# One operand sum of a seven-product matrix multiply, from GpSimd to VectorE in two halves

## Chip, cores and metric

One core of a Trainium2 chip. The metric is device time in microseconds (us) of one launch, the median of several runs; lower is better.

## What is computed

Pooled-query attention, then a gated feed-forward layer, all from the reference:

```python
q_pool = q.reshape(B, H, S // 2, 2, D).mean(axis=3)        # B=H=8, S=1152, D=64
scores = scale * q_pool @ k^T ;  attn = softmax(scores) ;  x = attn @ v     # 4608 rows of 512
a = x @ w1 ; b = x @ w2                                    # 512 -> 1024 each
h = a * b @ w3 ; out = h @ w_out                           # 1024 -> 1024 -> 512
```

## The kernel before, in words

**Attention.** Heads go in 32 pairs. The scores of all pairs are one long row of columns, cut into 324 groups of 512 for both heads of a pair (`scores`, L423 to L437): TensorE writes a group into one of three PSUM buffers (tag `psc`), ScalarE takes its exponential into the ring `ring` (L437). 144 "AV" units (`av_mm`, L463; `av_norm`, L484 to L498) multiply the exponentials with v and divide by the sums, on TensorE and VectorE. `prepare` (L779), called once for each pair, puts a batch of four GpSimd instructions in that engine's queue: the casts and sums of k (L344), q (L348, L350) and v (L357). GpSimd works its queue in order, and so does VectorE.

**Feed-forward.** The two last weights are multiplied once into T (1024 x 512). The 4608 rows then go in nine chunks of 512 (`moe_groups`). For each chunk, 16 projections (`proj`, L578, alternately by w1 and w2) and their gates (L695) fill the tile gT: [128 partitions, 8 feature tiles, 512 rows] in fp16. gT times T is done with seven products of half-size blocks instead of eight. With the four blocks of gT (feature tiles 0-3 or 4-7, rows 0-255 or 256-511) named a11, a12, a21, a22, each 1024 columns wide in a partition, the left operands are

- s1 = a21 + a22, by VectorE, four instructions of 256 columns, one after each of the last four gates (L608)
- a21 becomes a11 - a21, by GpSimd, four instructions beside those (L609)
- a11 becomes s1 - a11, **the second operand sum**, one instruction of 1024 columns (L616), by GpSimd, and by VectorE only where `tail[0]` is set, that is in the last two chunks
- a12 becomes a12 - a11, one instruction of 1024 columns by GpSimd (L618)

The products (L678, eight matmuls each) run in the order 1, 2, 5, 6, 7, 4, 3. Product 1 reads the old a11, 2 the old a12, 5 reads s1, 6 the new a11, 7 the new a21, 4 reads a22, 3 the new a12. The result of each leaves PSUM through VectorE (`only` L641, `plus` L632; in the last two chunks `only` runs on ScalarE, L639), and two sums of results follow on GpSimd (L635).

**Order.** The projections and products are "fills", put between the attention work by hand. The 324 score groups make 108 visits of three. Each visit is three score groups on TensorE and then a string of items found by a search (`_visits`, L192): "A" is an AV unit, "m" a fill that goes into the single PSUM bank `mo`, "s" a fill that takes one of the three score buffers, "P" a transpose. The search tracks TensorE, ScalarE and VectorE with fixed costs; GpSimd is not in it. The list `fills` (L821 to L828) says for each fill how many PSUM-to-SBUF steps' worth of VectorE time it brings beyond the normal one (third entry). What is left after visit 108 runs as AV unit, fill, AV unit, fill and so on, and the two last chunks run alone as the tail.

The steps that the change touches: `s_rest` (L611), its calls in `done` (L650) after products 1 and 2, and the entries of `fills` for a chunk.

Of the kernel before, what the change touches and what calls it, by code (L numbers as in the profile page):

```python
# [11 lines left out]
ALU = mybir.AluOpType  # L12
# [244 lines left out]
def kernel(  # L257
# [11 lines left out]
    nc = tc.nc  # L269
# [7 lines left out]
    NF = dff // 128  # L277
# [243 lines left out]
    tail = [False]  # L521
# [34 lines left out]
    HF, HM, HC = NF // 2, dm // 2, 256  # L556
    TB = {}

    def t_sums():
        b11, b12 = T16[:, 0:HF, 0:HM], T16[:, 0:HF, HM:dm]  # L560
        b21, b22 = T16[:, HF:NF, 0:HM], T16[:, HF:NF, HM:dm]
        ts = msb.tile([128, 4, HF, HM], FP16, tag="wo", bufs=1, name="tsum")
        for o, x, y in ((0, b12, b11), (1, b22, ts[:, 0]), (2, b22, b12), (3, b21, ts[:, 1])):
            nc.gpsimd.tensor_tensor(out=ts[:, o], in0=x, in1=y, op=ALU.subtract)
        TB.update({1: b11, 2: b21, 3: b22, 4: ts[:, 3], 5: ts[:, 0], 6: ts[:, 1], 7: ts[:, 2]})
# [9 lines left out]
    def proj(pw, wt, ft, c):  # L575
        for mc in range(NC):
            for (d0, a, n) in runs(c):
                nc.tensor.matmul(pw[:, d0:d0 + n], wt[:, mc, ft * 128:ft * 128 + 128], xT[:, mc, a:a + n],  # L578
                                 start=(mc == 0 and d0 == 0), stop=(mc == NC - 1), skip_group_check=True)

    def store(eng, pos, osb):
        b, r = pos // (2 * Sq) * 2, pos % (2 * Sq)
        if r == QM * 128:
            for u in range(2):
                r0 = (b + u) * Sq + QM * 128
                eng.dma_start(out=out[r0:r0 + QT, :], in_=osb[u * QT:u * QT + QT, :])
            return
        if r > QM * 128:
            b, r = b + 1, r - QM * 128 - 2 * QT
        eng.dma_start(out=out[b * Sq:b * Sq + QM * 128, :].rearrange("(p c) n -> p c n", c=QM)[:, r // 128, :], in_=osb)  # L590
# [3 lines left out]
    def moe_groups(c):  # L594
        t = {}

        def left(n):
            g = t["g"]
            lo, hi = slice(0, HC), slice(HC, CH)
            return {1: g[:, 0:HF, lo], 2: g[:, HF:NF, lo], 3: g[:, HF:NF, lo], 4: g[:, HF:NF, hi],  # L600
                    5: t.get("s1"), 6: g[:, 0:HF, lo], 7: g[:, 0:HF, hi]}[n]

        def s_pair(f):
            g = t["g"]
            if f == 0:
                t["s1"] = msb.tile([128, HF, HC], FP16, tag="s1", bufs=1, name="s1")
            a11, a21, a22 = g[:, f, 0:HC], g[:, f, HC:CH], g[:, HF + f, HC:CH]
            nc.vector.tensor_tensor(out=t["s1"][:, f], in0=a21, in1=a22, op=ALU.add)  # L608
            nc.gpsimd.tensor_tensor(out=a21, in0=a11, in1=a21, op=ALU.subtract)  # L609

        def s_rest(n):  # L611
            g = t["g"]
            a11, a12 = g[:, 0:HF, 0:HC], g[:, HF:NF, 0:HC]
            if n == 2:
                eng = nc.vector if tail[0] else nc.gpsimd
                eng.tensor_tensor(out=a11, in0=t["s1"], in1=a11, op=ALU.subtract)  # L616
            else:
                nc.gpsimd.tensor_tensor(out=a12, in0=a12, in1=a11, op=ALU.subtract)  # L618

        IS = 1.0 / (SCL * SCL)  # L620

        def part(name):
            t[name] = msb.tile([128, 2, HM], FP32, tag="t2k", bufs=4, name=name)
            return t[name]

        def rows(h):
            if h not in t:
                t[h] = msb.tile([128, 2, dm], FP32, tag="osb", bufs=2, name="osb")
            return t[h]

        def plus(out, pt, x):
            nc.vector.scalar_tensor_tensor(out=out, in0=pt, scalar=IS, in1=x, op0=ALU.mult, op1=ALU.add)  # L632

        def add(out, x, y):
            nc.gpsimd.tensor_tensor(out=out, in0=x, in1=y, op=ALU.add)  # L635

        def only(out, pt):
            if tail[0]:
                nc.scalar.mul(out=out, in_=pt, mul=IS)  # L639
            else:  # L640
                nc.vector.tensor_scalar_mul(out=out, in0=pt, scalar1=IS)  # L641

        def out_rows(h, u):
            if tail[0]:
                eng = nc.scalar if c in final and u else nc.sync
            else:
                eng = nc.gpsimd
            store(eng, c * CH + h * HC + u * 128, rows(h)[:, u, :])

        def done(n, pt):  # L650
            if n == 1:
                only(part("p"), pt)
                s_rest(2)
            elif n == 2:
                plus(rows(0)[:, :, 0:HM], pt, t["p"])
                s_rest(4)
            elif n == 5:
                only(part("q"), pt)
            elif n == 6:
                plus(t["p"], pt, t["p"])  # L660
                add(part("w"), t["p"], t["q"])
            elif n == 7:
                plus(part("z"), pt, t["p"])
                add(rows(1)[:, :, HM:dm], t["z"], t["q"])
            elif n == 4:
                plus(rows(1)[:, :, 0:HM], pt, t["z"])
                for u in range(2):
                    out_rows(1, u)
            else:
                for u in range(2):  # L670
                    plus(rows(0)[:, u, HM:dm], pt[:, u, :], t["w"][:, u, :])
                    out_rows(0, u)

        def product(pt, n, tiles=(0, 1)):
            a, b = left(n), TB[n]
            for u in tiles:
                for f in range(HF):
                    nc.tensor.matmul(pt[:, u, :], a[:, f, u * 128:u * 128 + 128], b[:, f, :],  # L678
                                     start=(f == 0), stop=(f == HF - 1))

        def first(pa, ft):
            if ft == 0:
                t["g"] = msb.tile([128, NF, CH], FP16, tag="g8", bufs=2, name="gT")
            proj(pa, w1sb, ft, c)

        def keep(pa):
            t["a"] = msb.tile([128, CH], FP32, tag="t2k", bufs=4, name="asb")
            if tail[0]:
                nc.scalar.copy(out=t["a"], in_=pa)  # L689
            else:  # L690
                nc.vector.tensor_copy(out=t["a"], in_=pa)  # L691

        for ft in range(NF):
            def gate(pb, ft=ft):
                nc.vector.tensor_tensor(out=t["g"][:, ft, :], in0=pb, in1=t["a"], op=ALU.mult)  # L695
                if ft >= HF:
                    s_pair(ft - HF)
                if ft == 0 and not TB:
                    t_sums()

            yield 1, lambda pa, ft=ft: first(pa, ft), keep, 0.0
            yield 1, lambda pb, ft=ft: proj(pb, w2sb, ft, c), gate, 0.0
        order7 = (1, 2, 5, 6, 7, 4, 3)
        for i, n in enumerate(order7):
            def go(po, n=n, i=i):
                near[0] = c in final and i >= 3
                product(po.rearrange("p (u m) -> p u m", u=2), n)

            def put(po, n=n):
                done(n, po.rearrange("p (u m) -> p u m", u=2))  # L710

            def go_last(po, n=n):
                for u in range(2):
                    pu = ps.tile([128, 2, 512], FP32, tag="psc", bufs=3, name="mol")[:, 0:2, 0:HM]
                    product(pu, n, (u,))
                    plus(rows(0)[:, u, HM:dm], pu[:, u, :], t["w"][:, u, :])
                    out_rows(0, u)

            if c in final and c == max(final) and n == order7[-1]:
                yield 1, go_last, None, 0.0  # L720
            else:
                yield 1, go, put, 0.0
# [28 lines left out]
    def w_load(dst, src):  # L751
# [7 lines left out]
        out=ident16, in_=ident16, compare_op=ALU.not_equal, fill=1.0,  # L759
# [46 lines left out]
    for c in range(B * Sq // CH):  # L806
        n = 0
        for b in range(B):
            for t in range(NT5):
                if xpos(b, t) < (c + 1) * CH and xpos(b, t) + (128 if t < QM else QT) > c * CH:  # L810
                    p = b * HP + HP - 1
                    i = unit_of(p, t)
                    n = max(n, i + 2, index[(p, QM - 1)] + 1 + HELD if p >= XD and t < QM else 0)
# [7 lines left out]
    fills = []  # L821
# [2 lines left out]
    free = []  # L824
    for n in range(NU + 1):
        for c in loose.get(n, []):
            fills += [(1, 0.0, 0.0)] * NF + [(1, 0.0, 0.0), (1, 0.0, 0.25)] * HF + [(1, 0.0, 0.0)] * 7
        free.append(len(fills))  # L828
    turn = {}
    for p in range(1, NPE):  # L830
# [121 lines left out]
```

## Time and profile before

| | |
|---|---|
| median of three runs | 420.89 us (420.61 to 423.12) |
| the profiled execution | 420.94 us, of which span 419.2 us |
| second operand sum L616 on GpSimd | 7 x 2.12 us, at 102.2 to 362.0 us |
| second operand sum L616 on VectorE | 2 x 0.69 us, at 386.4 and 406.6 us |
| L618 on GpSimd | 9 x 2.12 us |
| L608 on VectorE (256 columns) | 36 x 0.292 us (0.291 to 0.367) |
| L609 on GpSimd (256 columns) | 36 x 0.667 us |
| a GpSimd batch L344, L348, L350, L357 | 1.15, 1.27, 0.45 and 1.14 us |
| a VectorE step out of PSUM (L641, L632, L695) | 0.69 us |
| a product of eight matmuls | 0.87 us of TensorE, start to start |

How to read it: the span runs from the first to the last instruction of the program. A view of the profile is the page (sums), the waits (which engine waited for which, in total, number of times, longest), or the timeline (instructions in order: start, busy time, engine, line, operation, and in brackets the idle time of the engine before it and what ended it).

### The profile page before, as it was taken

Reading aid. Unit: us, or ns where it says so; the run is one execution under the profiler, and the core shown is the slowest. Engines: PE = TensorE matmul, PEld = TensorE weight load, DVE = VectorE, ACT = ScalarE, POOL = GpSimd, SP = SyncE. Lnnn points to the kernel's source line nnn. Section 1 sums busy time; section 2 is a strip of 40 time slices with the busy share of each in tenths; the row PEclk is TensorE's granted clock in tenths of the full one; section 3 lists DMA queues with packets and bytes.
Section 4 is the critical chain, followed back from the end, with each engine's and each line's share of the span. In section 5 each row is a group of like instructions: output and inputs, shape, how many; then the busy total and the mean of one; then the engine's idle time right before and its main releaser. Section 6 shows DMA issues by size and latency. Waiting matters only on the chain.

```text
span 419.2 us, 13307 instructions
## 1 busy us (share of the span) xinstructions
PE 394.9 (94%) x5545; PEld 268.1 (64%) x5545; DVE 236.3 (56%) x643; ACT 322.0 (77%) x347; POOL 253.9 (61%) x284
## 2 busy tenths in 40 slices
PE   3899999999999999999999999979998999989992
PEld 1477786566766676658666866567776755745561
DVE  1156665666565655565556555745564556765552
ACT  4988988998899898989998989869996896023230
POOL 5899868937971689069906890598158501522333
PEclk9999999999999999999999999999998999999997
DMA  8999998499799999979999999699976420030302
GB/s 272 250 316 317 299 295 302 156 278 262 200 315 269 253 174 284 232 210 244 301 252 278 225 255 255 174 270 242 311 118 111 95 80 14 14 114 1 100 2 107
DMA packets 90963, 86.39 MB, mean 206 GB/s; under 512 B 59664, under 2 KB 64272, under 8 KB 90896
## 3 DMA queue, kind: packets, MB, share of 16 engines
q1 hardware_dynamic: 81600, 59.32, 58.8%
q0 software_dynamic: 8720, 25.10, 20.9%
q10 hardware_dynamic: 576, 1.05, 0.7%
q8 instruction: 44, 0.72, 0.7%
q14 instruction: 23, 0.19, 0.2%
HBM read 67.11 MB, written 9.44 MB: 183 GB/s over the span
## 4 chain that ended last, share of the span: by engine, by line
PE 85%; DVE 4%; POOL 3%; ACT 3%; issue 2%; DMA 1%; POOLq 1%; ACTq 0%; DVEq 0%
PE psc L432 19%; PE avb L463 16%; PE mot L578 16%; PE mo L578 14%; PE mot L678 5%; PE mo L678 5%; ACT ring L437 3%; PE mo L545 3%; PE avb L460 2%; PE ptk L372 2%; DVE gT L695 1%; POOL gT L616 1%; DMA qst<-in_q_dram 1%; PE mot L545 1%; DVE kqT L374 1%
## 5 line engine op out<-in xcount | busy, mean ns | idle before, releaser
L437 ACT ACTIVATE ring<-psc 128x1024 f16<-128x1024 f32 x324 | 308.1, 1025 | 38.8 <-PE psc L432 37.6
L609 POOL TENSOR_TENSOR gT<-gT 128x256 f16<-128x256 f16 x36 | 24.0, 667 | 129.3 <-DVE s L608 71.3
L432 PE MATMUL psc<-kqT 64*128 64x512 f16 (+7 forms) x1152 | 96.5, 291 | 4.5 <-ACT ring L437 1.5
L463 PEld LDWEIGHTS <-ring 128*128 128x128 f16 x2304 | 84.8, 98 | 21.3 <-issue 8.9
L463 PE MATMUL avb<-vaug,ring 128*128 128x65 f16 x2304 | 91.8, 194 | 0.2
L432 PEld LDWEIGHTS <-kqT 64*128 64x128 f16 x1152 | 46.3, 95 | 31.9 <-issue 9.3
L678 PEld LDWEIGHTS <-gT 128*128 128x128 f16 x432 | 40.3, 98 | 13.5 <-POOL gT L616 4.9
L578 PEld LDWEIGHTS <-w1sb 128*128 128x128 f16 x320 | 28.3, 98 | 30.9 <-issue 6.7
L484 DVE RECIPROCAL rzall<-avb 128x2 f32<-128x2 f32 x144 | 23.8, 165 | 40.2 <-PE avb L463 21.5
L578 PEld LDWEIGHTS <-w2sb 128*128 128x128 f16 x320 | 28.3, 98 | 28.3 <-issue 4.6
L578 PE MATMUL mot<-xT,w2sb 128*128 128x512 f16 (+1 forms) x196 | 42.2, 344 | 0.0
L578 PE MATMUL mot<-xT,w1sb 128*128 128x512 f16 x156 | 40.0, 379 | 1.5 <-DVE z L632 1.5
L348 POOL TENSOR_TENSOR kq<-qst 128x512 f16<-128x512 f32 x31 | 39.4, 1271 | 1.4 <-DMA qst<-in_q_dram 1.4
L695 DVE TENSOR_TENSOR gT<-mot,asb 128x512 f16<-128x512 f32 x41 | 28.4, 692 | 18.3 <-PE mot L578 18.0
L689 ACT COPY asb<-mot 128x512 f32<-128x512 f32 x16 | 9.4, 585 | 37.9 <-PE mot L578 20.1
L344 POOL CAST kq<-kst 128x1152 f16<-128x1152 f32 x31 | 35.6, 1148 | 3.8 <-DMA kst<-in_k_dram 3.3
L357 POOL CAST vaug<-vst 128x1152 f16<-128x1152 f32 x32 | 36.6, 1143 | 0.5 <-DMA vst<-in_v_dram 0.5
L691 DVE COPY asb<-mo 128x512 f32<-128x512 f32 x33 | 22.8, 691 | 24.5 <-PE mo L578 24.3
L695 DVE TENSOR_TENSOR gT<-mo,asb 128x512 f16<-128x512 f32 x31 | 21.4, 692 | 25.7 <-PE mo L578 25.6
L578 PE MATMUL mo<-xT,w1sb 128*128 128x512 f16 (+2 forms) x164 | 34.2, 339 | 0.0
L578 PE MATMUL mo<-xT,w2sb 128*128 128x512 f16 x124 | 32.0, 381 | 0.0
L498 DVE TENSOR_TENSOR xb<-avb,rzall 128x128 f16<-128x128 f32 x96 | 28.0, 292 | 3.3
(100 smaller groups left out, 421.8 us busy)
## 6 DMA issues: line engine op xcount, KB each, us to landing
vst<-in_v_dram SPq DMA_DIRECT2D x25, 576.0 KB, 4.9
kst<-in_k_dram SPq DMA_DIRECT2D x23, 576.0 KB, 5.6
qst<-in_q_dram SPq DMA_DIRECT2D x23, 512.0 KB, 6.7
out_dram<-osb POOLq DMA_DIRECT2D x21, 256.0 KB, 6.1
kst<-in_k_dram POOLq DMA_DIRECT2D x8, 576.0 KB, 9.3
qst<-in_q_dram POOLq DMA_DIRECT2D x8, 512.0 KB, 10.1
vst<-in_v_dram POOLq DMA_DIRECT2D x7, 576.0 KB, 6.6
out_dram<-osb SPq DMA_DIRECT2D x9, 256.0 KB, 2.5
```

The source lines that it names most:

```text
L344: nc.gpsimd.tensor_copy(out=kq16[:, 0:NJ].rearrange("p c u d -> p u c d"), in_=kst.rearrange("p u (c d) -> p u c d", d=D))
L348: eng.tensor_tensor(out=kq16[:, NJ:NJ + QM].rearrange("p c u d -> p u c d"), in0=qv[:, :, :, 0], in1=qv[:, :, :, 1], op=ALU.add)
L357: nc.gpsimd.tensor_copy(out=va[:, :, :, 0:D], in_=vs.pop(p).rearrange("p u (c d) -> p u c d", d=D))
L432: nc.tensor.matmul(psc[:, u, f - s * G:f - s * G + ln], kT2[u * 64:u * 64 + 64, jt, :], qpT[u * 64:u * 64 + 64, i0:i0 + ln], start=True, s ...
L437: nc.scalar.activation(out=ring[:, :, r0:r0 + G], in_=psc, func=AF.Exp, bias=0.0, scale=SCALE)
L463: nc.tensor.matmul(avb[:, o + u * E1:o + u * E1 + E1], ring[:, u, c0:c0 + 128], va[:, u, jt, :], start=(jt == 0 and u == 0), stop=(jt == N ...
L484: nc.vector.reciprocal(out=rzall[:, i, :], in_=av[:, :, D:E1].rearrange("p u o -> p (u o)"))
L498: nc.vector.tensor_tensor(out=xbt, in0=av[:, :, 0:D], in1=rzall[:, i, :].unsqueeze(2).to_broadcast([128, 2, D]), op=ALU.mult)
L578: nc.tensor.matmul(pw[:, d0:d0 + n], wt[:, mc, ft * 128:ft * 128 + 128], xT[:, mc, a:a + n], start=(mc == 0 and d0 == 0), stop=(mc == NC - ...
L609: nc.gpsimd.tensor_tensor(out=a21, in0=a11, in1=a21, op=ALU.subtract)
L678: nc.tensor.matmul(pt[:, u, :], a[:, f, u * 128:u * 128 + 128], b[:, f, :], start=(f == 0), stop=(f == HF - 1))
L695: nc.vector.tensor_tensor(out=t["g"][:, ft, :], in0=pb, in1=t["a"], op=ALU.mult)
```

## The change

The second operand sum of every chunk goes to VectorE as two instructions of 512 columns: feature tiles 0 and 1 after the result of product 1 has been taken, tiles 2 and 3 after that of product 2. L618 is issued behind the second half as before. The planner's list counts more VectorE time for products 1 and 2 (0.45 each) and for the last four gates of a chunk (0.30 in place of 0.25), so that the search gives another order of fills in some visits. The number of visits, and the 173 fills that fall into them, stay.

```diff
         def s_rest(n):
             g = t["g"]
             a11, a12 = g[:, 0:HF, 0:HC], g[:, HF:NF, 0:HC]
-            if n == 2:
-                eng = nc.vector if tail[0] else nc.gpsimd
-                eng.tensor_tensor(out=a11, in0=t["s1"], in1=a11, op=ALU.subtract)
+            if n < 2:
+                h = slice(n * HF // 2, (n + 1) * HF // 2)
+                nc.vector.tensor_tensor(out=a11[:, h], in0=t["s1"][:, h], in1=a11[:, h], op=ALU.subtract)
             else:
                 nc.gpsimd.tensor_tensor(out=a12, in0=a12, in1=a11, op=ALU.subtract)
...
             if n == 1:
                 only(part("p"), pt)
-                s_rest(2)
+                s_rest(0)
             elif n == 2:
                 plus(rows(0)[:, :, 0:HM], pt, t["p"])
+                s_rest(1)
                 s_rest(4)
...
-            fills += [(1, 0.0, 0.0)] * NF + [(1, 0.0, 0.0), (1, 0.0, 0.25)] * HF + [(1, 0.0, 0.0)] * 7
+            fills += [(1, 0.0, 0.0)] * NF + [(1, 0.0, 0.0), (1, 0.0, 0.3)] * HF + [(1, 0.0, 0.45)] * 2 + [(1, 0.0, 0.0)] * 5
```

## The prediction, made before the changed kernel ran

> **What bounds the kernel now.** First the page, for who is busy.
>
> ```profile
> PE 394.9 (94%) x5545; PEld 268.1 (64%) x5545; DVE 236.3 (56%) x643; ACT 322.0 (77%) x347; POOL 253.9 (61%) x284
> PE 85%; DVE 4%; POOL 3%; ACT 3%; issue 2%; DMA 1%; POOLq 1%; ACTq 0%; DVEq 0%
> ```
>
> TensorE is busy for 394.9 of 419.2 us and carries 85% of the chain that ended last; GpSimd (POOL) carries 3%. So a change pays only where TensorE stands still. Next the waits, for whether the moved sum ever holds TensorE:
>
> ```profile
> PEld L678 <- POOL gT L616: 4.9, 2, 2.5
> PE mot L678 <- POOL gT L616: 4.3, 2, 2.3
> ```
>
> The columns are total us, times, longest us. It does, twice: in two of the seven chunks that use GpSimd (weight load and matmul are two views of the same two waits). In the other five nobody waits for L616. Then the timeline of the second, to see why:
>
> ```profile
> 315.82 2.85 ACT L437 ACTIVATE ring<-psc 128x1024 f16<-128x1024 f32 x3 [0.48 <-PE psc L432]
> 315.83 0.67 POOL L609 TENSOR_TENSOR gT<-gT 128x256 f16<-128x256 f16 x1 [2.51 <-DVE rzall L484]
> ...
> 316.44 1.15 POOL L344 CAST kq<-kst 128x1152 f16<-128x1152 f32 x1
> ...
> 319.05 2.86 ACT L437 ACTIVATE ring<-psc 128x1024 f16<-128x1024 f32 x3 [0.37 <-PE psc L432]
> ...
> 319.17 1.14 POOL L357 CAST vaug<-vst 128x1152 f16<-128x1152 f32 x1
> ...
> 320.28 2.11 POOL L616 TENSOR_TENSOR gT<-s,gT 128x1024 f16<-128x1024 f16 x1
> ...
> 322.44 1.86 PE L678 MATMUL mot<-tsum,gT 128*128 128x256 f16 x8 [2.08 <-POOL gT L616]
> ...
> 326.21 5.61 ACT L437 ACTIVATE ring<-psc 128x1024 f16<-128x1024 f32 x6 [4.31 <-PE psc L432]
> ```
>
> The sum L616 is queued on GpSimd behind a whole batch of casts (316.44 to 320.31), and product 6 needs it. The first wait, near 277 us, is the same picture. ScalarE's rows give the price, since each row of three exponentials is one visit: 319.05 to 326.21 is 7.16 us where the visit before took 3.23 (315.82 to 319.05), an excess of 3.93. It is more than the idle time because the eight matmuls behind it took 1.86 us instead of the usual 1.05: the granted clock was 0.53 from 322.4 to 324.3 us and 0.50 in the next microsecond, and 1.00 before. The other visit lasted 5.59 (275.76 to 281.35) against 3.21 for the one before it: 2.38, with the clock at 1.00.
>
> **The change, part by part.** The sum is made against the profiled execution, 420.94 us (span 419.2 and 1.74 around it; the median is 420.89, or 0.05 less).
>
> *The two waits go.* 3.93 + 2.38 = 6.31 us. The visits right behind are some 0.12 shorter than others of their kind (2.73 and 2.83 against 2.85 to 2.95), a catching-up that goes too: 6.31 - 0.25 = 6.06. What is late next there is nothing of size: without these two, TensorE has no gap over 0.3 us from 28 to 368 us, and the sums stand well ahead of product 6 once they need no batch. GpSimd loses 7 x 2.12 = 14.9 us of work; L618 comes forward by up to that 2.12, but product 3, its reader, is the last of seven and waits nowhere now, so that is worth nothing.
>
> *VectorE's own time.* 256 columns take 0.292 (L608) and 1024 take 0.692 (L616 in the tail), so 512 take 0.292 + 256 x 0.400/768 = 0.425. Fourteen halves are 5.95 us more on an engine that is 56% busy. A visit with product 1 holds two PSUM steps (1.38), L608 (0.29), a half (0.43) and one AV unit (0.45) at most, about 2.6 of 3.2 us: it fits, and I cost the bare time at nothing. If the cover failed it would be that 5.95. In the stretch without exponentials (352 to 367 us), where VectorE is at 12.4 of 15 us, its idle pieces between 362 and 366 sum to about 1.2 us against the 0.85 of the two halves.
>
> *VectorE held by GpSimd.* The halves read two SBUF operands, as L608 does. Six times L608 met a running L348; the timeline shows one:
>
> ```profile
> 221.13 1.27 POOL L348 TENSOR_TENSOR kq<-qst 128x512 f16<-128x512 f32 x1
> ...
> 222.18 0.37 DVE L608 TENSOR_TENSOR s<-gT 128x256 f16<-128x256 f16 x1
> 222.36 0.50 POOL L350 TENSOR_TENSOR kq<-qtl 64x128 f16<-64x128 f32 x1
> ```
>
> L608 ended 0.15 us after L348 did (222.55 against 222.40), whenever it had started; so in all six, and L350 took 0.50 instead of 0.45. L900 in the tail, a VectorE instruction beside L635, took 1.384 where its twin L899 took 0.300. So I take it that a half which meets a cast is held to the cast's end and then needs 0.15 + 256 x 0.52 ns = 0.28; a hold is between 0 and 1.27 (a whole L348). The place matters. The changed order puts a batch right behind L609 in chunks 1, 3 and 4 (counting from 0); with the rows of the present trace as clock:
> - Chunk 3: the result of product 1 is taken at 230.97, L348 runs 230.75 to 232.02. First half held to 232.30 (about 0.9), the result step of product 2 to 232.99, second half held by L357 to about 234.1. The changed order puts product 5 right behind 2 in that visit, in `mo`. Behind the halves on VectorE stand the result steps of products 2 and 5 and an AV unit; the third score group waits for the buffer of product 2 (233.06 against 232.5, 0.55), product 6 for `mo` (234.87 against 233.9, 0.97). TensorE loses 1.5.
> - Chunk 1: second half held from 146.88 to 147.48, a score buffer late: 0.2. Chunk 4: halves held 0.1 and 0.2, hidden under an AV unit: 0.
> - Chunk 5: here the changed order puts the batch between the third and the fourth L609, and the second half needs the fourth: a new wait of VectorE for GpSimd. The batch lasts 3.87 (316.44 to 320.31) from the third L609, and the fourth gate comes one visit (3.2) later, so the fourth L609 is some 1.5 late; by then VectorE has two result steps and the first half to do and stands about 0.1 to 0.6: 0.3.
>
> In chunks 0, 2 and 6 no batch meets the halves. Together 2.0 us. Bounds: 0 (all halves fall between casts) and eight halves x 1.27 = 10.2. I take a value near the rows that place them.
>
> *The new order of fills.* No fill leaves or enters the visits, so TensorE's work stays. In four visits two "m" fills now stand around one "s"; from the last matmul to the bank's next one are 0.18 (the usual bracket of L632 behind L678), 0.69 and 0.06 (VectorE's end at 407.26, TensorE's start at 407.32), 0.93, and the fill between takes 0.87: 4 x 0.06 = 0.25. Bounds: 0 and 4 x 0.69.
>
> *The last two chunks.* One sum of 0.69 becomes two of 0.425, the second behind the result step of product 2 and behind the fourth L609 (405.87 to 406.54). The whole sum ended at 407.26 and product 6 stood 0.31 for it. Now its first matmuls can start on the first half, the third needs the second half, which ends at about 407.4 to 407.8. Between -0.3 and +0.5 each; I take +0.1 each, 0.2. L618 follows by the same, with 0.4 to spare before product 3.
>
> Sum: -6.06 + 0 + 2.0 + 0.25 + 0.2 = -3.6; 420.94 - 3.6 = 417.3 us. Without the fills' and the holds' terms it would be 415.1.
>
> A page of the Trainium skill speaks against the change: "SBUF — State Buffer", section "Who interferes with whom", says that a VectorE instruction with two SBUF inputs contends with a GpSimd instruction that reads SBUF, and that the later one is blocked for the whole of the other. By that rule, put on every half near a batch, the sum would be that of the third rival. The six rows of L608 agree with it.
>
> **Rivals.**
> 1. *Nothing is given back*: the halves fall between casts. For it: L608 met a cast in only 6 of 36 cases, and at most 0.075 us was lost. Against: in chunk 3 the half stands in the middle of L348. 420.94 - 6.06 + 0.2 = 415.1.
> 2. *The wait changes its engine*: in chunk 5 VectorE stands for the fourth L609 through the whole batch, with an AV unit and the result step of product 5 behind it, and TensorE waits for their banks. For it: the order, and that a batch has stopped TensorE twice. Against: the batch starts as soon as GpSimd is free, a visit early; its loads kept GpSimd waiting 3.3 us in all (L344, twice). 417.3 + 3.9 = 421.2, no change.
> 3. *Slower: VectorE is held in all eight halves of chunks 1, 3, 4 and 5 by a whole cast*, and TensorE, whose banks VectorE empties, loses it one for one: 420.94 - 6.06 + 10.2 + 0.45 = 425.5. It decides against the change from a mean of 5.6/8 = 0.70 us for each half that reaches TensorE. For it: the batches are unbroken, 3.9 us long. Against: VectorE has idle time in those visits, and in chunk 4 the halves just slip past.
>
> That the change does not do what it says is not a rival: the order has no L616 left on GpSimd.
>
> **How the numbers follow.** Forecast 0.60, rival 1 0.15, rival 2 0.15, rival 3 0.10. Range: 414.3 (rival 1 with the tail at its bound, 415.1 - 0.2 - 0.6) to 421.2 (rival 2), which leaves out rival 3 and some of rival 2. A change of 1% is about what a measurement of this kernel can tell from none: below 416.7 is faster, above 425.1 slower. The forecast lies 0.6 above the first edge, and of its spread (415.3 to 419.5) I put 0.4 below it: faster 0.24 + 0.15 = 0.39; slower 0.07, most of rival 3; same 0.54.
>
> **What would show it.** Right: no wait of L678 for L616 or any GpSimd line near 277 and 320 us; the visits there 3.2 us long; the clock at 1.00 there; halves of 0.425, with some of 0.7 to 1.4 that end 0.28 after a cast, in chunk 3 above all, followed by TensorE waiting 1 to 1.5 us for VectorE's L632 or L641. Wrong: halves of 0.425 beside running casts (then the holds' term is nothing), a wait of VectorE for L609 of some 4 us, or a new gap of TensorE over 1 us elsewhere.

## The result, and the profile after

| | before | changed |
|---|---|---|
| median of nine runs | 422.28 us (420.61 to 424.15) | 418.75 us (418.56 to 419.91) |
| profiled execution, its span | 420.94, 419.2 us | 418.71, 416.9 us |
| ratio, 95% interval | | 0.9923 (0.9898 to 0.9948) |

The change makes the kernel 0.77% faster. The interval leaves out 1, so this is clear of noise, though it is less than the 1% that the prediction took for the least that can be told from none. A second series of six runs gave 0.9937 (0.9918 to 0.9956). The nine runs before lie in two groups, four at 420.6 to 421.1 us and five at 422.3 to 424.2, which is not explained here; the profiled execution is of the lower group, so the medians differ by 3.53 us and the two profiled executions by 2.23.

The page of the changed kernel, the same two lines as before (busy time by engine, and the chain that ended last):

```profile
PE 394.8 (95%) x5545; PEld 267.3 (64%) x5545; DVE 244.4 (59%) x659; ACT 322.0 (77%) x347; POOL 241.0 (58%) x277
...
PE 86%; DVE 6%; ACT 2%; issue 1%; DMA 1%; POOLq 1%; POOL 0%; ACTq 0%; DVEq 0%
```

GpSimd has left the chain (3% to 0%), and VectorE's share has grown from 4% to 6%. VectorE's busy time grew by 8.1 us. The eighteen halves (L616) take 11.48 us by their own durations, where 0.415 each would be 7.47: for about 4 us VectorE was held. The waits of TensorE alone, in us, times, longest, show who took GpSimd's place:

```profile
PE mo L679 <- DVE osb L632: 0.8, 1, 0.8
...
PE mo L679 <- DVE q L641: 0.6, 1, 0.6
PE psc L432 <- DVE osb L632: 0.3, 1, 0.3
```

No product waits for L616 on GpSimd any more (the products are now L679, the file being one line longer). Three new waits for VectorE stand there. The timeline of VectorE and TensorE in chunk 3 has two of them:

```profile
231.84 1.41 DVE L616 TENSOR_TENSOR gT<-s,gT 128x512 f16<-128x512 f16 x1
233.17 0.68 DVE L632 SCALAR_TENSOR_TENSOR osb<-mot,p 128x512 f32<-128x512 f32 x1
...
233.77 1.16 DVE L616 TENSOR_TENSOR gT<-s,gT 128x512 f16<-128x512 f16 x1
...
233.90 0.39 PE L432 MATMUL psc<-kqT 64*128 64x512 f16 x2 [0.35 <-DVE osb L632]
...
235.58 1.03 PE L679 MATMUL mo<-tsum,gT 128*128 128x256 f16 x8 [0.64 <-DVE q L641]
```

The halves take 1.41 and 1.16 us there, against 0.41 where nothing meets them. Behind the first stands the result step of product 2, for whose buffer the third score group waits; behind the second that of product 5 (`q`, L641), for whose bank `mo` product 6 waits. The third wait is in chunk 5, where product 5 waits for the bank of a result step (L632) that stands behind the first half:

```profile
318.22 1.14 POOL L357 CAST vaug<-vst 128x1152 f16<-128x1152 f32 x1
318.48 1.79 DVE L616 TENSOR_TENSOR gT<-s,gT 128x512 f16<-128x512 f16 x1
...
319.32 0.66 POOL L609 TENSOR_TENSOR gT<-gT 128x256 f16<-128x256 f16 x1
...
320.92 1.03 PE L679 MATMUL mo<-tsum,s 128*128 128x256 f16 x8 [0.79 <-DVE osb L632]
```

**Where the time went, by visits.** A visit is taken here from the start of its first exponential to that of the next visit's. The table sums them by stretches; a stretch named for a chunk holds that chunk's fills (the bounds are visits 24, 34, 48, 62, 76, 90, 104). Every number is us of one profiled execution; the last column is what is left to the end of the span. The kernels from the third row on are the experiments below.

| kernel | to visit 24 | chunk 0 | 1 | 2 | 3 | 4 | 5 | 104 to 107 | rest |
|---|---|---|---|---|---|---|---|---|---|
| before | 84.98 | 31.79 | 43.44 | 43.47 | 43.94 | 45.83 | 47.82 | 9.50 | 68.40 |
| changed | 85.31 | 32.09 | 43.67 | 43.55 | 45.30 | 43.80 | 44.85 | 9.51 | 68.85 |
| order_only | 86.31 | 32.19 | 43.43 | 43.55 | 47.72 | 43.80 | 43.91 | 9.51 | 69.05 |
| move_only | 86.12 | 31.80 | 43.73 | 43.73 | 47.55 | 44.35 | 44.86 | 9.50 | 68.94 |
| late_batch_before | 85.48 | 31.80 | 43.43 | 43.46 | 43.93 | 43.42 | 44.09 | 9.50 | 68.47 |
| late_batch_after | 85.08 | 32.09 | 43.44 | 43.55 | 45.23 | 43.80 | 43.92 | 9.51 | 68.95 |
| late_batch_move | 85.89 | 31.80 | 43.44 | 43.75 | 44.74 | 43.43 | 44.09 | 9.51 | 68.85 |
| late_batch_order | 86.04 | 32.19 | 43.44 | 43.56 | 44.44 | 43.81 | 43.91 | 9.51 | 68.33 |
| one_whole | 85.18 | 32.09 | 43.70 | 43.67 | 44.77 | 44.51 | 45.30 | 9.51 | 68.65 |
| write_only | 86.49 | 32.09 | 43.67 | 43.55 | 43.99 | 43.80 | 44.87 | 9.51 | 68.94 |

The first column is the same instructions in all ten kernels and still differs by 1.5 us, so it says nothing of the change. From the second on, a stretch with the same instructions repeats within some 0.1 us, but for the last column: order_only has 69.05 there and the other kernels with the sum whole on GpSimd 68.33 to 68.47. TensorE's last instruction ends at the same time in them, 60.2 us after the start of visit 107, so this difference lies behind it. The changed kernel gained 2.03 in chunk 4 and 2.97 in chunk 5, and gave back 0.30, 0.23, 0.08 and 1.36 in chunks 0 to 3 and 0.45 in the rest.

### The profile page after: what moved, and what is told of

The parts are those of the page before. It is cut to its first block, busy times and chain, and to the rows that moved or that the text cites. A ratio compares the mean times of both kernels' runs of the same rounds, so it can differ in the third digit from the quotient of the medians.

```text
span 416.9 us, 13305 instructions
## 1 busy us (share of the span) xinstructions
PE 394.8 (95%) x5545; PEld 267.3 (64%) x5545; DVE 244.4 (59%) x659; ACT 322.0 (77%) x347; POOL 241.0 (58%) x277
## 4 chain that ended last, share of the span: by engine, by line
PE 86%; DVE 6%; ACT 2%; issue 1%; DMA 1%; POOLq 1%; POOL 0%; ACTq 0%; DVEq 0%
PE psc L432 20%; PE avb L463 16%; PE mot L578 16%; PE mo L578 15%; PE mo L679 6%; PE mot L679 4%; PE mo L545 3%; PE avb L460 3%; ACT ring L437 2%; PE ptk L372 2%; DVE gT L616 1%; DVE osb L632 1%; DVE kqT L374 1%; DMA qst<-in_q_dram 1%; PE mot L545 1%
## 5 line engine op out<-in xcount | busy, mean ns | idle before, releaser
L609 POOL TENSOR_TENSOR gT<-gT 128x256 f16<-128x256 f16 x36 | 24.3, 675 | 120.8 <-DVE s L608 89.0
L578 PE MATMUL mot<-xT,w1sb 128*128 128x512 f16 (+1 forms) x216 | 49.3, 355 | 1.5 <-DVE z L632 1.5
L696 DVE TENSOR_TENSOR gT<-mo,asb 128x512 f16<-128x512 f32 x42 | 29.1, 692 | 36.6 <-PE mo L578 36.4
L679 PEld LDWEIGHTS <-gT 128*128 128x128 f16 x432 | 40.4, 98 | 9.1 <-issue 2.4
L344 POOL CAST kq<-kst 128x1152 f16<-128x1152 f32 x31 | 36.0, 1163 | 13.2 <-DMA kqT<-kq 9.7
L578 PE MATMUL mo<-xT,w2sb 128*128 128x512 f16 (+1 forms) x200 | 43.5, 347 | 0.0
L348 POOL TENSOR_TENSOR kq<-qst 128x512 f16<-128x512 f32 x31 | 39.4, 1272 | 1.4 <-DMA qst<-in_q_dram 1.4
L357 POOL CAST vaug<-vst 128x1152 f16<-128x1152 f32 x32 | 36.6, 1145 | 0.4 <-DMA vst<-in_v_dram 0.3
L578 PE MATMUL mot<-xT,w2sb 128*128 128x512 f16 x120 | 30.8, 379 | 0.0
L696 DVE TENSOR_TENSOR gT<-mot,asb 128x512 f16<-128x512 f32 x30 | 20.8, 692 | 16.4 <-PE mot L578 16.2
L498 DVE TENSOR_TENSOR xb<-avb,rzall 128x128 f16<-128x128 f32 x96 | 28.0, 292 | 3.3
L618 POOL TENSOR_TENSOR gT<-gT 128x1024 f16<-128x1024 f16 x9 | 19.1, 2124 | 11.4 <-DVE rzall L484 7.6
L692 DVE COPY asb<-mo 128x512 f32<-128x512 f32 x24 | 16.6, 691 | 14.4 <-PE mo L578 13.9
```

What stands on the lines that cost most here:

```text
L344: nc.gpsimd.tensor_copy(out=kq16[:, 0:NJ].rearrange("p c u d -> p u c d"), in_=kst.rearrange("p u (c d) -> p u c d", d=D))
L348: eng.tensor_tensor(out=kq16[:, NJ:NJ + QM].rearrange("p c u d -> p u c d"), in0=qv[:, :, :, 0], in1=qv[:, :, :, 1], op=ALU.add)
L357: nc.gpsimd.tensor_copy(out=va[:, :, :, 0:D], in_=vs.pop(p).rearrange("p u (c d) -> p u c d", d=D))
L498: nc.vector.tensor_tensor(out=xbt, in0=av[:, :, 0:D], in1=rzall[:, i, :].unsqueeze(2).to_broadcast([128, 2, D]), op=ALU.mult)
```

## The experiments

The theory to test: the gain is two waits behind a batch of casts, ended by taking the sum out of GpSimd's queue; what is given back is VectorE held by GpSimd. Rivals: the new order of fills does it; the bare time of the halves is what costs.

**order_only**: the kernel before with the new entries of `fills`, the sum whole on GpSimd.

```diff
-            fills += [(1, 0.0, 0.0)] * NF + [(1, 0.0, 0.0), (1, 0.0, 0.25)] * HF + [(1, 0.0, 0.0)] * 7
+            fills += [(1, 0.0, 0.0)] * NF + [(1, 0.0, 0.0), (1, 0.0, 0.3)] * HF + [(1, 0.0, 0.45)] * 2 + [(1, 0.0, 0.0)] * 5
```

> The new order of fills alone; the sum stays whole on GpSimd, as before. Theory (the gain is the two waits, each ended by moving the sum out of the queue behind a batch, and the order of fills is worth little): under the new order chunk 4 still puts product 6 behind the batch and the sum, so its wait of 2.3 us stays; chunk 5 now has product 6 a visit later, so its 3.9 us go; chunk 3 has product 6 earlier, which makes a new wait of up to 1.6 us: 420.9 - 3.9 + 1.6 + 0.3 = 418.9 us. Rival A (the engine does it all): both old waits stay, 421.2. Rival B (the order does it all): both are gone and no wait of L679 or L678 for L616 is left, 417 or less.

Measured: median 419.14 us, ratio 0.9938 (0.9914 to 0.9963), about the gain of the whole change. The total was expected, the way was not: both old waits are gone, that of chunk 4 too, because the new order has product 1 a visit earlier and so issues L616 ahead of the batch. Chunk 3 has a new wait that costs 3.8 us (47.72 against 43.94), twice what was expected. GpSimd and TensorE in the timeline:

```profile
234.20 1.14 POOL L357 CAST vaug<-vst 128x1152 f16<-128x1152 f32 x1
235.30 2.10 POOL L616 TENSOR_TENSOR gT<-s,gT 128x1024 f16<-128x1024 f16 x1
...
237.46 1.38 PE L678 MATMUL mo<-tsum,gT 128*128 128x256 f16 x8 [2.17 <-POOL gT L616]
```

It is the picture of the two old waits in another chunk, and again the matmuls behind it are slow (granted clock 0.75 from 236 to 240 us and 0.82 from 240 to 244). The order alone removes two waits and makes one. The intervals show no difference between the order alone and the whole change.

**move_only**: the changed kernel with the old entries of `fills`.

```diff
-            fills += [(1, 0.0, 0.0)] * NF + [(1, 0.0, 0.0), (1, 0.0, 0.3)] * HF + [(1, 0.0, 0.45)] * 2 + [(1, 0.0, 0.0)] * 5
+            fills += [(1, 0.0, 0.0)] * NF + [(1, 0.0, 0.0), (1, 0.0, 0.25)] * HF + [(1, 0.0, 0.0)] * 7
```

> The two halves on VectorE, with the old order of fills. Theory: the waits of chunks 4 and 5 go (-6.06), and the halves are held by batches in chunks 3, 4 and 5, each costing TensorE 0.8 to 0.9 through the score buffer of product 2, chunk 1 0.2, tail 0.4: 420.94 - 6.06 + 2.6 + 0.2 + 0.4 = 418.1 us. Rival (holds of VectorE do not reach TensorE; what was given back came from the new order): 415.3. Rival A (order does it all): 421 or more.

Measured: 421.15 us, ratio 0.9974 (0.9950 to 0.9998): nearly nothing, 3 us above the expectation. It is the time that rival A gave, but not by its way: both waits for L616 are gone, and the holds reach TensorE. Chunks 4 and 5 give back 0.9 and 0.8 us (44.35 and 44.86 against 43.42 and 44.09 without a batch in the way), as expected; chunk 3 gives back 3.6, four times the figure (0.3 of it without any hold, as late_batch_move shows below). The waits of TensorE:

```profile
PE psc L432 <- DVE osb L632: 2.1, 3, 0.8
...
PE avb L463 <- DVE xb L498: 1.1, 1, 1.1
```

In chunk 3 an AV unit stood behind the second held half on VectorE, and TensorE waited for it too. The window view of that stretch, whose columns are the busy time and number of instructions of PE, PEld, DVE, ACT and POOL, then the granted clock, the DMA share and GB/s:

```profile
232.00:236.00 4.00, 2.32 (x36) 1.74 (x34) 3.96 (x6) 3.69 (x5) 3.58 (x5) 1.00 0.96 270
236.00:240.00 4.00, 3.87 (x48) 3.01 (x49) 1.51 (x6) 0.64 (x1) 1.94 (x1) 0.57 0.59 199
```

Behind two waits of 0.72 and 1.09 us close together the granted clock was 0.57 for the next four. So the move without the new order falls into the holds.

**late_batch_after** and **late_batch_before**: the changed kernel and the kernel before, each with four batches issued behind the items of their visit instead of ahead of them, and nothing else.

```diff
+    LATE = {43: 43, 70: 70, 84: 84, 97: 97}
+    held = []
...
                 if 0 < pn < NP - 2:
-                    prepare(pn + 2)
+                    if vis in LATE:
+                        held.append(pn + 2)
+                    else:
+                        prepare(pn + 2)
...
             else:
                 assert fill(what == "s")
+        if held and vis in LATE.values():
+            prepare(held.pop(0))
```

> The changed kernel, with the GpSimd batch of casts issued behind the items of the visit in four visits (43, 70, 84, 97; those beside products 1 and 2 of chunks 1, 3, 4 and 5), so that no half meets a batch. Theory (the give-back is VectorE held by GpSimd): every half takes 0.41 to 0.52, the long visits of chunk 3 (4.15) and chunk 5 (4.06) fall to 2.9, 418.7 - 1.3 - 1.15 = 416.2 us. Rival (the give-back is the order of fills or the bare time of the halves): 418.7, unchanged.

> The kernel before, the sum whole on GpSimd and the old order of fills, with the same four batches issued behind the items of their visits, so that the sum stands in front of the batch. Theory (the cause of the two waits is the place in the queue, not GpSimd's 2.12 us): both waits go, 420.94 - 6.06 = 414.9 us, faster than the changed kernel. Rival (GpSimd is too slow for the sum): waits for L616 stay, 419 or more.

Measured: late_batch_after 417.34 us, ratio 0.9902 (0.9869 to 0.9934). Every half takes 0.41 to 0.51 us. Visit 71 falls from 4.15 to 2.83 and visit 98 from 4.06 to 3.11, so the holds cost 1.3 and 0.95 us, and in chunk 1 0.23. The median missed the expected 416.2 by 1.1 us. A new wait stands there, in visit 74, which takes 4.63 instead of 3.40:

```profile
245.46 0.38 PE L578 MATMUL mo<-xT,w1sb 128*128 128x512 f16 x1 [1.08 <-DMA xT<-xb]
```

The pair's loads are issued behind its casts, so they now went out at 236.1 instead of 231.8 us, close ahead of the transpose of x that chunk 4 needs. That this is the cause is not shown: late_batch_before sends them as late (236.3) and has no such wait.

late_batch_before: 415.66 us, ratio 0.9868 (0.9823 to 0.9913). Its timeline in chunk 5:

```profile
315.37 2.13 POOL L616 TENSOR_TENSOR gT<-s,gT 128x1024 f16<-128x1024 f16 x1 [0.78 <-PE mo L678]
...
318.27 1.04 PE L678 MATMUL mot<-tsum,gT 128*128 128x256 f16 x8
```

The sum, still 2.13 us on GpSimd, ends at 317.50, and product 6 starts at 318.27 behind no wait (no bracket); the batch's first cast, L344, follows at 319.65. The two waits were the place in the queue, not the engine's speed. Against the kernel before, chunks 4 and 5 are shorter by 2.41 and 3.73 us: 6.14 together. The median is 0.8 above the expected 414.9; in the profiled executions the first column alone is 0.5 longer.

**late_batch_move** and **late_batch_order** put the late batches on move_only and on order_only (the diffs are those above).

> Halves on VectorE, old order of fills, the four batches issued behind the items of their visits. Theory (what the move of the sum costs is the meeting with a batch, not VectorE's 5.95 us of bare time): halves of 0.41 to 0.52, the visits that were long with the halves alone (6.47 in chunk 3, 4.10 in chunk 4, 4.21 in chunk 5) fall to 2.9 to 3.4, and the time is that of the same kernel with the sum on GpSimd and late batches, 415.7, plus 0.4 in the tail: 416.1 us. Rival (bare time on VectorE reaches TensorE): 418 or more.

> Sum whole on GpSimd, new order of fills, late batches. Theory (the order matters only by where it puts sum, batch and product 6): no wait for L616; the new wait of chunk 3 that the order alone made (visit of 6.17) falls to 2.9; the wait of a projection for the transposed x after chunk 3 (1.2 us with late batches and this order) may come back: 416.0 to 417.2 us. Rival (this order needs the sum on VectorE): a wait of 1 us or more for L616 stays, 418 or more.

Measured: 416.78 us, ratio 0.9869 (0.9823 to 0.9915), and 416.28 us, ratio 0.9855 (0.9809 to 0.9901). No product waits for L616 in either. Against late_batch_before, the halves on VectorE cost 0.29 us in chunk 2, where a batch still meets them in the old order, 0.4 in the rest, and 0.8 in chunk 3; in chunks 0, 1, 4 and 5 they cost 0.01 or less. Of the 0.8, 0.49 is visit 74, where TensorE waits 0.34 for x as above (late_batch_order, without halves, has 0.45 more there too). The other 0.30 is visit 71, where no GpSimd instruction meets the halves and TensorE waits for an AV unit's step (L498) behind the second one:

```profile
233.03 0.42 DVE L616 TENSOR_TENSOR gT<-s,gT 128x512 f16<-128x512 f16 x1
...
233.56 0.29 DVE L498 TENSOR_TENSOR xb<-avb,rzall 128x128 f16<-128x128 f32 x1
...
233.91 0.71 PE L463 MATMUL avb<-vaug,ring 128*128 128x65 f16 x18 [0.25 <-DVE xb L498]
```

So in the old order their bare time is hidden but for this 0.30. In the new order (late_batch_after against late_batch_order) no visit from 24 to 106 is longer by it but visit 74, the one with the wait for x. With the batch out of the way neither engine nor order is worth a difference that these intervals can show.

**one_whole**: the changed kernel with the sum as one instruction of 1024 columns on VectorE after product 1.

```diff
-            if n < 2:
-                h = slice(n * HF // 2, (n + 1) * HF // 2)
-                nc.vector.tensor_tensor(out=a11[:, h], in0=t["s1"][:, h], in1=a11[:, h], op=ALU.subtract)
+            if n == 0:
+                nc.vector.tensor_tensor(out=a11, in0=t["s1"], in1=a11, op=ALU.subtract)
...
-                s_rest(1)
```

> The changed kernel with the sum in one instruction of 1024 columns on VectorE after product 1. Theory: one hold instead of two in chunk 3 (visit 71 from 4.15 to about 3.5); in chunk 5 the whole sum waits for the fourth L609 and holds the result of product 2, visit 98 from 4.06 to 4.2 to 4.4; tail 0.3 shorter: 418.0 us, no change that shows. Rival (the split is what makes the change pay): 419.5 or more.

Measured: 419.28 us, ratio 0.9943 (0.9917 to 0.9970), 1.3 above the expectation and 0.2 below the rival's 419.5. Chunk 3 is 0.53 shorter than with halves (one hold of 1.67), chunks 4 and 5 are 0.71 and 0.45 longer: the whole sum waits for the fourth L609, and in chunk 4 it is then held to 1.60. The rest is 0.2 shorter. The split gains in some places what it loses in others, and the intervals show no difference from the changed kernel.

**write_only**: the changed kernel with the batch beside chunk 3 replaced by fills with zero; k, q and v of one pair each are left out.

```diff
         kq16 = kq16s[p % 2]
+        if p == 23:
+            nc.gpsimd.memset(kq16[:, 0:NJ], 0.0)
+            nc.gpsimd.memset(kq16[:, 0:NJ + QM], 0.0)
+            nc.gpsimd.memset(kq16[0:QT, NJ + QM], 0.0)
+            pairs[p] = kq16
+            return
...
+        if p == 22:
+            vs.pop(p)
+            nc.gpsimd.memset(va[:, :, :, 0:D], 0.0)
+            return
```

> The changed kernel, with the four GpSimd instructions of the batch beside chunk 3 replaced by fills with zero of the same tiles (and one of a longer stretch), so that GpSimd only writes there; the k, q and v of one pair each are left out. Theory (a half is held because GpSimd reads SBUF at that time): the halves of chunk 3 take 0.41 to 0.52 beside running fills and visit 71 falls from 4.15 to 2.9. Rival (any running GpSimd instruction holds a half, or its writes do): halves that meet a fill take longer and end with it.

Measured, in one profiled execution (line numbers are ten higher):

```profile
232.88 1.48 POOL L346 MEMSET kq<- 128x1664 f16 x1
...
233.02 0.42 DVE L626 TENSOR_TENSOR gT<-s,gT 128x512 f16<-128x512 f16 x1
```

This half and the next, at 233.95, begin inside a GpSimd instruction that only writes, and take 0.42 us each. Visit 71 is 2.83. So it is GpSimd's reading that holds a half, not its being busy; this was shown for one batch.

**after_again** and **late_batch_before_again**: the same two kernels once more, on one chip.

> The changed kernel once more, unchanged. Theory: the same holds at the same places, since the order is fixed: in chunk 3 two halves of about 1.4 and 1.16 us, visit 71 of about 4.15; in chunk 5 a first half of about 1.8 us that outlasts both L357 and the fourth L609, visit 98 of about 4.06; ratio to the kernel before 0.990 to 0.995. Rival (the holds are chance): other lengths, or none.

> The kernel before with the four batches issued behind the items of their visits, once more, on the same chip as the changed kernel. Theory (the place in GpSimd's queue is the cause, and leaving the sum on GpSimd spares the holds and 0.4 us of the tail): no wait for L616; ratio 0.984 to 0.989, 2 to 3 us below the changed kernel. Rival (the two versions are worth the same): the same ratio as the changed kernel within 0.003.

Measured: 0.9937 (0.9918 to 0.9956) and 0.9853 (0.9830 to 0.9875), medians 419.15 and 415.71 us. The intervals are apart. The holds came back to the hundredth: halves of 1.404 and 1.155 us in chunk 3 and 1.793 in chunk 5. late_batch_before beats both kernels.

## Why the prediction was right, and where its steps were off

The forecast was 417.3 us and the range 414.3 to 421.2; 418.75 lies in it, 1.45 above the forecast. The two waits went, and VectorE was held mostly where the prediction put the holds; but the prediction gave the engine alone the credit for the first, and that was wrong. The forecast change of -3.6 us was summed against the profiled execution, and the two profiled executions differ by -2.23. That the medians differ by -3.53, nearly the forecast, is luck: the median before was 420.89 from three runs and 422.28 from nine. The range is also wide, 7 us: a time without any change, 420.94, would have lain in it too. By its steps, with "no wait, no hold" taken from the late-batch kernels:

- *The two waits go*: right in size, -6.06 against -6.14 (2.41 and 3.73), the slow clock behind the second among it. But the step gave all of it to the engine. order_only shows that the new order by itself ends both, and move_only that the move by itself does. What the engine does in that order is to end the third wait, in chunk 3, that the order makes: 47.72 falls to 45.30. So the size came out right with some luck.
- *VectorE's own time, 0*: right for the visits of the new order (late_batch_after against late_batch_order), while the old order pays 0.30 in one visit (late_batch_move). Wrong for the stretch of AV units and fills without exponentials, where the step laid 1.2 us of idle pieces against 0.85 of halves: the first of the two last chunks starts 0.25 later.
- *VectorE held by GpSimd, 2.0*: right in kind and in place, 2.5 measured. Chunk 3: 1.5 forecast, 1.3 measured, with the second half, the score buffer and `mo` as described. Chunk 1: 0.2 and 0.23. Chunk 4: 0 and 0. Chunk 5: 0.3 and 0.95; this is the term most mis-sized. The step had the second half stand for the fourth L609; instead the first half, begun beside L357, was held to the end of that and of the fourth L609, 1.79 us in all, and the second half waited for nothing. In write_only, where the batch of chunk 3 only writes, the holds there are gone: a half takes 0.42 inside a fill of 1.48. The Trainium skill, "SBUF — State Buffer", section "Who interferes with whom", says that a VectorE instruction with two SBUF inputs contends with a GpSimd instruction that reads SBUF and not with one that only writes it; these rows agree.
- *The new order, 0.25*: about 0.65: 0.30 in chunk 0, 0.1 each in chunks 2 and 3 at most, 0.20 in chunks 4 and 5 together (87.71 against 87.51 without waits). That it is the 0.06 for each bank, as the step has it, is not shown.
- *The last chunks, 0.2*: 0.45 in the last column. Of it 0.25 is the late start just named. TensorE's last instruction ends 0.35 later, so the two last chunks themselves cost about 0.1. The last 0.1 lies behind that, where order_only differs by 0.6 from kernels with the same instructions, and may be chance.

The terms so far sum to -6.14 + 2.5 + 0.65 + 0.45 = -2.5; the profiled executions differ by -2.23, with 0.33 of start on top, which is chance. Rival 1 (nothing given back) fell with the holds. Rival 2 was half right: the fourth L609 behind a batch does hold VectorE, but by running beside the first half and not because the second half needs it, and for 0.95 us and not 3.9, since the batch had begun a visit earlier. Rival 3 (slower) came nearest in move_only, where six halves were held, for 1.15 to 1.43 us each, and nearly the whole gain was given back.

Not settled: what of the 0.30 in chunk 0 is the longer visit 24 and what visit 28, what makes the transpose of x late in some kernels with late batches, and why the half in chunk 5 lost its turn to L609.

## What to carry to other kernels

When an engine that works its queue in order makes TensorE wait, look first at what stands ahead of the instruction in that queue: putting the batch behind it gained twice as much here as moving the instruction to a faster engine. A planner that does not model the engine can remove a wait and make another by a small change of its costs, so a change of plan and a change of engine have to be tried apart. Before an elementwise instruction with two SBUF operands goes to VectorE, lay it beside what GpSimd reads at that time, and name what stands behind it.

## What the runs showed of the hardware that was not expected

- A VectorE instruction that meets a reading GpSimd instruction gets in at the end of it in some pairs, L609 before L344 and L348 before L350 (it ends 0.28 us later, and L344 takes 1.34 instead of 1.15, L350 0.63 instead of 0.45). At the end of L357 before L609 it did not, in three of three profiles with this order (changed, after_again, write_only): L609 ran first, and the half took 1.79.
- The clock fell after quite short idling: to 0.57 for some 4 us after waits of 0.72 and 1.09 us (move_only), and after one of 2.17 (order_only) and 2.08 (before), but not after one of 2.25 (before, 277 us). What decides it is not shown.
- The first 85 us, the same instructions in each kernel, took 84.98 to 86.49 us from one execution to another in the table above, as much as the smaller effects studied here.
